# Block-sparse attention and a feed-forward layer: the elementwise work of h - tanh(h) divided anew over ScalarE, GpSimd and VectorE

## The chip, the core and the metric

The kernel runs on one core of a Trainium2 chip. A core has a matrix engine (TensorE, PE in the profile, with its weight loads as PEld), three engines for elementwise work (VectorE as DVE, ScalarE as ACT, GpSimd as POOL), and a queue for transfers (SyncE, SP). Each engine works through its own instructions in order and waits for others by semaphores. The metric is the time of the whole program on the device in microseconds; less is better. Before the change the median of 3 runs is 1019.51 us (1017.39 to 1022.18).

## What is computed

```python
# attention: q, k, v of shape (4, 8, 768, 64), blocks of 32 positions
scores = scale * np.matmul(q, k.transpose(0, 1, 3, 2))
scores = np.where(mask, scores, -1e9)          # band, first and last blocks, three sampled blocks
attn = softmax(scores)
x = np.matmul(attn, v)                         # then as 3072 tokens x 512
# feed-forward layer: w_in 512 x 2048, w_out 2048 x 512
h = x @ w_in
g = h - np.tanh(h)
out = g @ w_out
```

The weights come as 64-bit floats. All products are made nearly exact: each operand is split into a high and a low part, and three products of parts are added.

## The kernel before, in words

**The attention** fills the first 437 us. It goes through 16 pairs of heads, and in each head through 6 tiles of 128 keys. `load` fetches k, q and v of a pair (tiles rawk, rawq, rawv). `prep_v` finds the largest absolute value of v (am, L212), turns it into a scale and writes v in two parts (vhl, L230 and L231). `smax` makes the row maxima (sm, mc, L245 and L246), `qk_exp` the scores and their exponentials, `split` the two parts of these (ph, pl), `accum` the product with v. The results go to memory as x.

**The feed-forward layer** goes through six chunks of tokens: the first has 2 parts of 3 tiles of 128 tokens, four have 4 tiles, the last has 2. The 2048 columns of h come as 16 tiles of 128, numbered ft. One *unit* is one part of a chunk and one ft, so the first chunk has 32 units of 384 tokens, the next four 16 units of 512 each, the last 16 units of 256. `first` (L496) makes h of a unit in PSUM with 12 products and then g; `second` (L533) multiplies g with w_out, two units later (LAG = 2).

Between them stands the elementwise work. With u = h*h, h - tanh(h) is h*u*C(u) with a cubic C where u is at most 0.16 (THR2), and the plain difference elsewhere. u (L514), tanh (t, L516) and a square of the cubic (qq, L518) are made on ScalarE; the mask mk = u > 0.16 (L520) on GpSimd; the product g = h*u (L522), the difference t = tanh(h) - h (L523), the two factors of the cubic (L524, L525) and the selection by the mask (L526) on VectorE. Then ScalarE rounds g to its high part gh (L529) and GpSimd makes the low part gl = g - gh (L530). L522 and L523 read h from PSUM; L524 to L526, L520 and L530 have all their tensors in SBUF.

**The weights** of ft 0 to 2 are prepared during the attention. Those of ft 3 to 15 are fetched as 64-bit words during the first chunk into four staging tiles; `convert` makes 32-bit floats of them with three VectorE instructions for each of w_in and w_out (L415, L418, L421: cvti and cvto), and `split_w` their two parts, the high on ScalarE (L476), the low on GpSimd (L478).

**What sets the order.** The program gives each part of the attention a due time in units of key tiles and emits by it; the feed-forward layer is emitted step by step in `step` (L555). A scheduler with a model of the engines' times then moves instructions within each engine's order. Buffers come from pools with a fixed count for each name: f2 holds u, t, qq, mk and g twice, gh and gl three times; h has two PSUM banks.

Of the kernel before, what the change touches and what calls it, by code (L numbers as in the profile page):

```python
# [11 lines left out]
F32 = mybir.dt.float32  # L12
# [4 lines left out]
AF = mybir.ActivationFunctionType  # L17
ALU = mybir.AluOpType
# [31 lines left out]
NH0, H0, DH = 2, 12 * NPAIR, 2  # L50
X0, DX = 175, 2

# order of the attention's parts, in key tiles relative to the product of scores
TQK, TV, TSM, LSP, LAV = -15.1, -5.6, -10.3, 2.1, 4.2
HPH, HPL = 29, 30
RS, RQ, RV, HR = 1, 2.5, 3, 6
# [1 line left out]
PL_DVE_END = (2, 5, 8, 11)  # L58
PH_DVE = (4,)

# h - tanh(h) = h * u * C(u), u = h * h, with the cubic C factored, for u <= THR2
THR2 = 0.16
C3 = -0.01988785306343693
CR = 2.604505935007862
# [7 lines left out]
@with_exitstack  # L72
def attention_ffn(ctx, tc, q, k, v, samp, w_in, w_out, blocks, out):
    nc = tc.nc
    cst = ctx.enter_context(tc.tile_pool(name="cst", bufs=1))
    dpool = ctx.enter_context(tc.tile_pool(name="dpool", bufs=1, space=DRAM))
    xscr = [dpool.tile([P, T, DM], F32, name=f"xscr{b}") for b in range(B)]

    ident = cst.tile([P, P], F32, name="ident")
    make_identity(nc, ident)  # L80
    qbias = cst.tile([P, 1], F32, name="qbias")
    nc.vector.memset(qbias, QB)

    big = ctx.enter_context(tc.tile_pool(name="ps_big", bufs=3, space=PSUM))
    one = ctx.enter_context(tc.tile_pool(name="ps_one", bufs=2, space=PSUM))
    ps = (
        lambda name: big.tile([P, 1024], F32, tag="big", name=name),
        lambda name: one.tile([P, 512], F32, tag="one", name=name),
    )
    slots = [cst.tile([P, 4, 2, S], F32R, name=f"slot{i}") for i in range(NSLOT)]  # L90
    wt = {(m, ft): dpool.tile([P, 512], F32, name=f"w{m}{ft}") for ft in range(NPRE) for m in "io"}
    f2 = ctx.enter_context(tc.tile_pool(name="f2", bufs=2))
    ffn = FFN(tc, w_in, w_out, xscr, ident, qbias, ps, slots, wt, out, f2)
    with ExitStack() as actx:
        attention(actx, tc, q, k, v, samp, w_in, w_out, blocks, xscr, ident, ps, slots, wt, f2, ffn)
    with ExitStack() as fctx:
        ffn.rest(fctx)


def attention(ctx, tc, q, k, v, samp, w_in, w_out, blocks, xscr, ident, ps, slots, wt, f2, ffn):  # L100
# [4 lines left out]
    vhl = [acst.tile([P, 2, T, 129], F16, name=f"vhl{i}") for i in range(NV)]  # L105
    onesrow = acst.tile([1, P], F32, name="onesrow")

    # operands of the scores, stacked over the contraction, for both heads of a pair:
    # sA = [kh; mask; 1], sB = [qh; one-hot; -max], sC = [kl; kh], sD = [qh; ql]
    sA, sB, sC, sD = ([slots[i][:, x] for i in range(NSLOT)] for x in range(4))  # L110

    loads = {}

    # transfers that the start waits for: the first pair's high parts, its low parts, its maxima
    urgent = [[], [], []]

    def after(n, d):
# [5 lines left out]
    def load(pr, which="kqv", first=None):  # L123
        b, hp = divmod(pr, H // 2)
        r = loads.setdefault(pr, [])
        for nm, src in ((n, x) for n, x in (("k", k), ("q", q), ("v", v)) if n in which):
            t = p2.tile([P, 2, T, D], F32, tag="raw" + nm, name=f"raw{nm}{pr}", bufs=3 if nm == "v" else 2)
            d = nc.sync.dma_start(out=t, in_=src[b, 2 * hp : 2 * hp + 2].rearrange("h (p t) d -> p h t d", t=T))
# [6 lines left out]
    def setup():  # L135
        nc.vector.memset(onesrow, 1.0)
        for i in range(NV):
            nc.vector.memset(vhl[i][:, :, :, 64:65], 1.0)
        # additive mask of query block x key block, expanded to the key columns, on partitions 64..87
        R = slice(64, 88)  # L140
        sp_i = acst.tile([P, 6], I32, name="sp_i")
        nc.sync.dma_start(out=sp_i[R, :], in_=samp)
        st_sb = acst.tile([P, 2 * NB + S], F32, name="st_sb")
        nc.sync.dma_start(out=st_sb[R, :], in_=blocks)
        oh = st_sb[:, 2 * NB : 2 * NB + S]
        sp_f = acst.tile([P, 3], F32, name="sp_f")
        nc.vector.tensor_copy(out=sp_f[R, :], in_=sp_i[R, :].rearrange("p (j w) -> p j w", w=2)[:, :, 0])
        allow = st_sb[R, 0:NB]
        for j in range(3):
            nc.vector.scalar_tensor_tensor(  # L150
                out=allow, in0=st_sb[R, NB : 2 * NB], scalar=sp_f[R, j : j + 1], in1=allow, op0=ALU.is_equal, op1=ALU.max
            )
        neg = acst.tile([P, NB], F32, name="neg")
        nc.vector.tensor_scalar(out=neg[R, :], in0=allow, scalar1=1.0, scalar2=-MASKED, op0=ALU.subtract, op1=ALU.mult)
        nat = p2.tile([P, S], F32, tag="pe", name="nat", bufs=4)
        mk = p2.tile([P, S], F32, tag="pe", name="mk", bufs=4)
        nc.vector.tensor_copy(
            out=nat[R, :].rearrange("p (n j) -> p n j", j=BLK), in_=neg[R, :].unsqueeze(2).to_broadcast([NB, NB, BLK])
        )
        for i in range(NSLOT):  # L160
            nc.gpsimd.memset(sA[i].bitcast(F32)[64:89], 1.0)
        for r in range(2):
            nc.vector.tensor_copy(
                out=mk[R, r * HS : (r + 1) * HS].rearrange("p (u c) -> p u c", u=3),
                in_=nat[R, :].rearrange("p (c u r) -> p r u c", u=3, r=2)[:, r],
            )
        return oh, mk
# [158 lines left out]
    ev = []  # L326

    def ramp(h, by):
        """how much less ahead a part is in the first heads"""
        return by * max(0, 1 - (h - 1) / HR) if h else 0  # L330

    def at(time, f, *args):
# [76 lines left out]


def convert(nc, pool, raw, name):
    """float64 words -> float32"""
    w = raw.rearrange("p (n w) -> p n w", w=2)
    t = pool.tile([P, 512], I32, tag="wcvt", name=name)
    nc.vector.tensor_scalar(  # L415
# [9 lines left out]


def split_x(nc, src, pt, xh, xl, ident):
    """the transpose of a tile of tokens, in high and low parts"""
    for c in range(NCT):
        nc.tensor.transpose(pt[:, c * P : (c + 1) * P], src[:, c * P : (c + 1) * P], ident)  # L430
    ptv = pt.rearrange("p (c n) -> p c n", c=NCT)
    nc.scalar.activation(out=xh, in_=ptv, func=AF.Copy)
    nc.vector.tensor_tensor(out=xl, in0=ptv, in1=xh.bitcast(F32), op=ALU.subtract)
# [7 lines left out]
class FFN:  # L441
    LAG = 2

    def __init__(self, tc, w_in, w_out, xscr, ident, qbias, ps, slots, wt, out, f2):
        self.nc = tc.nc
        self.tc = tc
        self.w_in, self.w_out, self.xscr, self.ident, self.qbias, self.wt, self.out, self.f2 = (
            w_in, w_out, xscr, ident, qbias, wt, out, f2
        )  # fmt: skip
        self.big, self.one = ps  # L450
        self.wi = [[None] * NFT, [None] * NFT]
        self.wo = [[None] * NFT, [None] * NFT]
        flat = [slots[(NPAIR - 3 + x) % NSLOT].rearrange("p a j s -> p (a j s)") for x in range(3)]
# [24 lines left out]
            eng.tensor_tensor(out=lo, in0=t, in1=hi.bitcast(F32), op=ALU.subtract)  # L478

    def fetch_x(self, n, j):  # L480
        """a tile of tokens of chunk n, loaded as it is"""
        if n == 1:
            raw = self.f2.tile([P, DM], F32, tag="wcvt", name=f"xn{n}_{j}")
        else:
# [11 lines left out]
    def first(self, n, s, ft):  # L496
# [13 lines left out]
        def tl(tag, dt=F32, **kw):  # L510
            return f2.tile([P, 512], dt, tag=tag, name=f"{tag}{n}_{s}_{ft}", **kw)[:, 0:w_]

        u = tl("u")
        nc.scalar.activation(out=u, in_=ph, func=AF.Square)  # L514
        t = tl("t")
        nc.scalar.activation(out=t, in_=ph, func=AF.Tanh)  # L516
        qq = tl("qq")
        nc.scalar.activation(out=qq, in_=u, func=AF.Square, scale=QS, bias=self.qbias)  # L518
        mk = tl("mk")
        nc.gpsimd.tensor_scalar(out=mk, in0=u, scalar1=THR2, scalar2=None, op0=ALU.is_gt)  # L520
        g = tl("g")
        nc.vector.tensor_tensor(out=g, in0=ph, in1=u, op=ALU.mult)  # L522
        nc.vector.tensor_tensor(out=t, in0=t, in1=ph, op=ALU.subtract)  # L523
        nc.vector.scalar_tensor_tensor(out=g, in0=u, scalar=CR, in1=g, op0=ALU.subtract, op1=ALU.mult)  # L524
        nc.vector.scalar_tensor_tensor(out=g, in0=qq, scalar=QC, in1=g, op0=ALU.add, op1=ALU.mult)  # L525
        nc.vector.copy_predicated(g, mk.bitcast(I32), t)  # L526
# [27 lines left out]

    def step(self):  # L555
        n, s, ft = self.units.pop(0)
        if s == 0:
            if n == 0 and ft + 2 < NFT and ft:
                self.split_w(ft + 2)
            if n == 0 and ft and ft + AHEAD < NFT:  # L560
                self.fetch_w(ft + AHEAD)
        nx = sum(CHUNKS[n + 1]) if n + 1 < len(CHUNKS) else 0
        if n and ft == 5:
            for j in range(nx):
# [1 line left out]
        if n and 0 <= ft - XF < nx:  # L566
            self.turn_x(n + 1, ft - XF)
        self.pend.append((n, s, ft, *self.first(n, s, ft)))
        if n == 0 and ft == NFT - 1:
            js = [j for j in range(nx) if j // 2 == s]  # L570
            for j in js:
                self.fetch_x(1, j)
# [56 lines left out]
```

## Time and profile before

| | |
|---|---|
| median of 3 runs | 1019.51 us (1017.39 to 1022.18) |
| span of the profiled execution, first to last instruction | 1019.9 us |
| the profiled execution's own time | 1019.9 us; the span is all that the profile gives of it |
| PE busy | 948.4 us, 93% |
| DVE busy | 786.0 us, 77% |
| ACT busy | 590.9 us, 58% |
| POOL busy | 637.0 us, 62% |

By stage, in busy us of the stretch:

| stretch (us) | what | PE | DVE | ACT | POOL |
|---|---|---|---|---|---|
| 0 to 437 | attention | 393.21 | 360.21 | 330.48 | 302.95 |
| 440 to 614 | first chunk | 151.79 | 156.77 | 76.87 | 126.30 |
| 614 to 962 | four chunks of 512 | 348.00 | 226.35 | 158.37 | 177.59 |
| 962 to 1020 | last chunk | 52.40 | 41.69 | 25.12 | 27.88 |

Busy means that an instruction had started and not ended, so time in which it stood still inside counts as busy. The granted TensorE clock is 0.98 to 1.00 of full speed in all four stretches.

### The profile page before, as it was taken

Reading aid. Unit: us, or ns where it says so; the run is one execution under the profiler, and the core shown is the slowest. Engines: PE = TensorE matmul, PEld = TensorE weight load, DVE = VectorE, ACT = ScalarE, POOL = GpSimd, SP = SyncE. Lnnn points to the kernel's source line nnn. Section 1 sums busy time; section 2 is a strip of 40 time slices with the busy share of each in tenths; the row PEclk is TensorE's granted clock in tenths of the full one; section 3 lists DMA queues with packets and bytes.
Section 4 is the critical chain, followed back from the end, with each engine's and each line's share of the span. In section 5 each row is a group of like instructions: output and inputs, shape, how many; then the busy total and the mean of one; then the engine's idle time right before and its main releaser. Section 6 shows DMA issues by size and latency. Waiting matters only on the chain.

```text
span 1019.9 us, 19428 instructions
## 1 busy us (share of the span) xinstructions
PE 948.4 (93%) x7472; PEld 795.2 (78%) x7472; DVE 786.0 (77%) x1261; ACT 590.9 (58%) x926; POOL 637.0 (62%) x436
## 2 busy tenths in 40 slices
PE   5888999999999999897888899999999999999997
PEld 3667877888788888785766678888888888888896
DVE  5689887878788888979899987666666756666676
ACT  1665887888888888744344444445444534543453
POOL 1564777777778777866877866545455544544554
PEclk9997999999999999999899999999999999999999
DMA  7987687777766757133233121011000100000010
GB/s 193 252 223 205 144 175 151 157 173 169 159 157 156 156 131 183 48 120 105 81 114 92 43 93 52 1 42 42 21 5 17 63 1 1 31 11 1 1 42 22
DMA packets 73549, 97.75 MB, mean 96 GB/s; under 512 B 5880, under 2 KB 63416, under 8 KB 73456
## 3 DMA queue, kind: packets, MB, share of 16 engines
q1 hardware_dynamic: 73456, 96.51, 37.4%
q8 instruction: 59, 0.97, 0.4%
q14 instruction: 34, 0.28, 0.1%
HBM read 43.59 MB, written 14.16 MB: 57 GB/s over the span
## 4 chain that ended last, share of the span: by engine, by line
PE 64%; DVE 18%; DMA 8%; issue 5%; ACT 2%; POOL 1%; SPq 1%; POOLq 0%; DVEq 0%; ACTq 0%
PE h L507 21%; PE o L545 7%; PE o L543 7%; PE o L544 7%; PE st L269 5%; PE sm L245 5%; PE st L270 4%; DMA slot<-hiq 4%; PE av L299 2%; DVE g L524 2%; PE av L306 2%; PE av L305 2%; DMA slot<-nm 2%; DVE rs L316 2%; DVE mc L246 2%
## 5 line engine op out<-in xcount | busy, mean ns | idle before, releaser
L284 POOL TENSOR_TENSOR pl<-pe,ph 128x768 f16<-128x768 f32 x173 | 294.8, 1721 | 132.6 <-ACT ph L282 98.1
L530 POOL TENSOR_TENSOR gl<-g,gh 128x512 fp32r<-128x512 f32 (+2 forms) x112 | 135.1, 1209 | 191.6 <-ACT gh L529 191.3
L246 DVE TENSOR_REDUCE mc<-sm 128x1 f32<-128x768 f32 x192 | 181.6, 950 | 49.6 <-PE sm L245 48.4
L272 ACT ACTIVATE pe<-st 128x768 f32<-128x768 f32 x192 | 154.4, 805 | 77.3 <-PE st L270 72.8
L529 ACT ACTIVATE gh<-g 128x512 fp32r<-128x512 f32 (+2 forms) x112 | 63.9, 571 | 219.8 <-DVE g L526 210.6
L520 POOL TENSOR_SCALAR mk<-u 128x512 f32<-128x512 f32 (+2 forms) x112 | 160.9, 1436 | 46.6 <-ACT u L514 39.8
L522 DVE TENSOR_TENSOR g<-h,u 128x512 f32<-128x512 f32 (+2 forms) x112 | 68.4, 611 | 127.1 <-ACT t L516 115.8
L269 PE MATMUL st<-slot 128*128 128x512 f32 (+1 forms) x384 | 145.4, 379 | 8.8 <-DVE mc L246 4.8
L282 ACT ACTIVATE ph<-pe 128x768 f16<-128x768 f32 x168 | 141.7, 843 | 4.5
L270 PE MATMUL st<-slot 89*128 89x512 f32 (+1 forms) x384 | 128.7, 355 | 4.9 <-DMA slot<-nm 4.9
L299 PE MATMUL av<-vhl,ph 128*128 128x65 f16 x1152 | 130.2, 195 | 0.6 <-DVE sc L220 0.6
L245 PE MATMUL sm<-slot 88*128 88x512 f32 (+1 forms) x384 | 114.6, 385 | 16.7 <-DMA slot<-hiq 12.5
L305 PE MATMUL av<-vhl,ph 128*128 128x64 f16 x1152 | 130.0, 196 | 0.0
L306 PE MATMUL av<-vhl,pl 128*128 128x65 f16 x1152 | 128.2, 194 | 0.1
L306 PEld LDWEIGHTS <-pl 128*128 128x128 f16 x1152 | 107.9, 100 | 10.8 <-issue 6.8
L299 PEld LDWEIGHTS <-ph 128*128 128x128 f16 x1152 | 108.3, 98 | 4.6 <-issue 1.1
L305 PEld LDWEIGHTS <-ph 128*128 128x128 f16 x1152 | 108.9, 98 | 2.3 <-issue 1.6
L543 PE MATMUL o<-wx,gh 128*128 128x512 f32 x240 | 96.0, 400 | 7.9 <-ACT gh L529 6.9
L507 PE MATMUL h<-slot,wx 128*128 128x384 f32 (+1 forms) x480 | 102.5, 363 | 0.5 <-DVE t L523 0.5
L269 PEld LDWEIGHTS st<-slot 128*128 128x128 f32 x384 | 76.0, 198 | 28.9 <-DVE mc L246 7.4
L545 PE MATMUL o<-wx,gl 128*128 128x512 f32 x240 | 92.0, 398 | 4.9 <-POOL gl L530 4.7
L514 ACT ACTIVATE u<-h 128x512 f32<-128x512 f32 (+2 forms) x112 | 59.7, 533 | 62.8 <-PE h L507 52.4
(108 smaller groups left out, 2021.8 us busy)
## 6 DMA issues: line engine op xcount, KB each, us to landing
slot<-hik SPq DMA_DIRECT2D x64, 192.0 KB
slot<-hiq SPq DMA_DIRECT2D x64, 192.0 KB
stage<-w_in SPq DMA_DIRECT2D x13, 512.0 KB
stage<-w_out SPq DMA_DIRECT2D x13, 512.0 KB
rawk<-k SPq DMA_DIRECT2D x16, 384.0 KB
rawq<-q SPq DMA_DIRECT2D x16, 384.0 KB
slot<-lok SPq DMA_DIRECT2D x32, 192.0 KB
slot<-loq SPq DMA_DIRECT2D x32, 192.0 KB
```

What stands on the lines that cost most here:

```text
L245: nc.tensor.matmul(pm[:, c], lhsT=sB[s][0:88, j, t * P : (t + 1) * P], rhs=sA[s][0:88, j, c], start=True, stop=True)
L246: nc.vector.tensor_reduce(out=mcs[h][:, t : t + 1], in_=pm[:, 0:S], op=ALU.max, axis=AX.X)
L269: nc.tensor.matmul(st[:, c], lhsT=sC[s][:, j, kc], rhs=sD[s][:, j, c], start=True, stop=False)
L270: nc.tensor.matmul(st[:, c], lhsT=sA[s][0:89, j, kc], rhs=sB[s][0:89, j, c], start=False, stop=True)
L284: d = eng.tensor_tensor(out=pl, in0=pe, in1=ph, op=ALU.subtract)
L299: m = nc.tensor.matmul(o[:, to, :], lhsT=ph[:, c], rhs=vv[:, 0:65], start=(kt == 0 and t == 0), stop=False, skip_group_check=True)
L305: nc.tensor.matmul(o[:, to, 0:64], lhsT=ph[:, c], rhs=vv[:, 65:129], start=False, stop=False, skip_group_check=True)
L306: nc.tensor.matmul(o[:, to, :], lhsT=pl[:, c], rhs=vv[:, 0:65], start=False, stop=last, skip_group_check=True)
L507: nc.tensor.matmul(ph, lhsT=w[:, cc], rhs=x[:, c, tk], start=(k == 0), stop=(k == 3 * NCT - 1))
L520: nc.gpsimd.tensor_scalar(out=mk, in0=u, scalar1=THR2, scalar2=None, op0=ALU.is_gt)
L543: nc.tensor.matmul(o, lhsT=gh[:, c], rhs=wo[0][ft], start=(ft == 0), stop=False)
L545: nc.tensor.matmul(o, lhsT=gl[:, c], rhs=wo[0][ft], start=False, stop=(ft == NFT - 1))
```

## The change

Six things change.

1. The mask is no longer a comparison on GpSimd but ReLU(u - 0.16) on ScalarE, with the bias in a new tile tbias. A positive number is not zero, so its bits select as before.
2. ScalarE also copies h from PSUM to SBUF: into a new tile hs for the first part of the first chunk (s = 0), into g's own tile in every other unit.
3. GpSimd makes g = h*u from that copy; VectorE's L522 is gone.
4. In the units of the first part of the first chunk, GpSimd also makes t = tanh(h) - h from hs; elsewhere VectorE makes it from PSUM as before.
5. `split_w(ft + 2)` is called after `first` of the second part of an ft instead of before `first` of its first part.
6. hs needs 2 x 384 floats of each partition (pool fh); the tile rawv of the attention has 2 buffers instead of 3.

```diff
-            t = p2.tile([P, 2, T, D], F32, tag="raw" + nm, name=f"raw{nm}{pr}", bufs=3 if nm == "v" else 2)
+            t = p2.tile([P, 2, T, D], F32, tag="raw" + nm, name=f"raw{nm}{pr}", bufs=2)
...
+    tbias = cst.tile([P, 1], F32, name="tbias")
+    nc.vector.memset(tbias, -THR2)
...
+    fh = ctx.enter_context(tc.tile_pool(name="fh", bufs=2))
...
         u = tl("u")
         nc.scalar.activation(out=u, in_=ph, func=AF.Square)
+        g = tl("g")
+        turn = n == 0 and s == 0
+        hs = self.fh.tile([P, w_], F32, tag="hs", name=f"hs{n}_{s}_{ft}") if turn else g
+        nc.scalar.activation(out=hs, in_=ph, func=AF.Copy)
         t = tl("t")
         nc.scalar.activation(out=t, in_=ph, func=AF.Tanh)
         qq = tl("qq")
-        nc.scalar.activation(out=qq, in_=u, func=AF.Square, scale=QS, bias=self.qbias)
+        nc.scalar.activation(out=qq, in_=u, func=AF.Square, scale=QS, bias=qbias)
         mk = tl("mk")
-        nc.gpsimd.tensor_scalar(out=mk, in0=u, scalar1=THR2, scalar2=None, op0=ALU.is_gt)
-        g = tl("g")
-        nc.vector.tensor_tensor(out=g, in0=ph, in1=u, op=ALU.mult)
-        nc.vector.tensor_tensor(out=t, in0=t, in1=ph, op=ALU.subtract)
+        nc.scalar.activation(out=mk, in_=u, func=AF.Relu, bias=tbias)
+        nc.gpsimd.tensor_tensor(out=g, in0=hs, in1=u, op=ALU.mult)
+        if turn:
+            nc.gpsimd.tensor_tensor(out=t, in0=t, in1=hs, op=ALU.subtract)
+        else:
+            nc.vector.tensor_tensor(out=t, in0=t, in1=ph, op=ALU.subtract)
...
     def step(self):
         n, s, ft = self.units.pop(0)
-        if s == 0:
-            if n == 0 and ft + 2 < NFT and ft:
-                self.split_w(ft + 2)
-            if n == 0 and ft and ft + AHEAD < NFT:
-                self.fetch_w(ft + AHEAD)
+        if s == 0 and n == 0 and ft and ft + AHEAD < NFT:
+            self.fetch_w(ft + AHEAD)
...
         self.pend.append((n, s, ft, *self.first(n, s, ft)))
+        if s == 1 and n == 0 and ft and ft + 2 < NFT:
+            self.split_w(ft + 2)
```

In the changed file the lines of `first` stand a little lower: u L519, the copy of h L523, tanh L525, qq L527, mk L529, h*u L530, the difference on GpSimd L532 and on VectorE L534, the cubic L535 and L536, the selection L537, gh L540, gl L541; the splits' low part is L482.

**GpSimd in the first chunk**, before: one ft, from the low part of unit (s 0, ft 8) on. A name such as gl_0_8 is the tile gl of part 0 and ft 8; the number behind it is the buffer's.

```order
L530 TENSOR_TENSOR gl_0_8_8690<-g_0_8_8683,gh_0_8_8689 128x384
L520 TENSOR_SCALAR mk_0_9_8775<-u_0_9_8769 128x384
L530 TENSOR_TENSOR gl_1_8_8730<-g_1_8_8723,gh_1_8_8729 128x384
L520 TENSOR_SCALAR mk_1_9_8815<-u_1_9_8809 128x384
L478 TENSOR_TENSOR wx_7959<-cvti_8742,wx_7958 128x512
L478 TENSOR_TENSOR wx_7961<-cvto_8748,wx_7960 128x512
L530 TENSOR_TENSOR gl_0_9_8784<-g_0_9_8777,gh_0_9_8783 128x384
```

And after, the same stretch:

```order
L541 TENSOR_TENSOR gl_0_8_8709<-g_0_8_8694,gh_0_8_8708 128x384
L530 TENSOR_TENSOR g_1_8_8736<-g_1_8_8736,u_1_8_8734 128x384
L530 TENSOR_TENSOR g_0_9_8791<-hs_0_9_8792,u_0_9_8789 128x384
L532 TENSOR_TENSOR t_0_9_8794<-t_0_9_8794,hs_0_9_8792 128x384
L482 TENSOR_TENSOR wx_7971<-cvti_8947,wx_7970 128x512
L482 TENSOR_TENSOR wx_7973<-cvto_8953,wx_7972 128x512
L541 TENSOR_TENSOR gl_1_8_8750<-g_1_8_8736,gh_1_8_8749 128x384
L541 TENSOR_TENSOR gl_0_9_8806<-g_0_9_8791,gh_0_9_8805 128x384
```

Each ft had two masks, two low parts and two splits; now it has two products, one difference, two low parts and two splits, every one an operation on two tensors.

**VectorE in the attention**, around the maximum am of the values of a later pair. Before:

```order
L212 TENSOR_REDUCE am_3298<-rawv_2324 128x1
L220 TENSOR_SCALAR sc_2341<-sc_2341 1x1
L246 TENSOR_REDUCE mc_2176<-sm_3_2264 128x1
L221 TENSOR_SCALAR sc_2341<-sc_2341 1x1
L280 CAST ph_4_2333<-pe_4_2258 128x768
L222 TENSOR_SCALAR sc_2341<-sc_2341 1x1
L225 TENSOR_SCALAR sc_2341<-sc_2341 1x1
L246 TENSOR_REDUCE mc_2176<-sm_4_2316 128x1
L246 TENSOR_REDUCE mc_2176<-sm_5_2352 128x1
L228 COPY sb_2348<-pa_2339 128x2
L246 TENSOR_REDUCE mc_2408<-sm_0_2409 128x1
L231 SCALAR_TENSOR_TENSOR vhl_97<-rawv_1363,sb_2348,vhl_97 128x12x64
```

After, from the same write of vhl (now L234) on:

```order
L234 SCALAR_TENSOR_TENSOR vhl_102<-rawv_1368,sb_2353,vhl_102 128x12x64
L249 TENSOR_REDUCE mc_2413<-sm_0_2414 128x1
L256 TENSOR_SCALAR nm_2363<-pmt_2361 6x128
L317 TENSOR_SCALAR rs_2494<-av_2284 128x6
L318 RECIPROCAL rs_2494<-rs_2494 128x6
L249 TENSOR_REDUCE mc_2413<-sm_1_2429 128x1
L319 TENSOR_SCALAR rs_2494<-rs_2494,sb_1871 128x6
L215 TENSOR_REDUCE am_3303<-rawv_2329 128x1
```

The read of rawv into am stood eleven rows ahead of the write of vhl for an earlier pair; now it stands seven rows behind it, and its buffer is the one that this write sets free.

**ScalarE in a chunk of 512 tokens**, before, two units:

```order
L529 ACTIVATE gh_0_7_9755<-g_0_7_9749 128x512
L514 ACTIVATE u_0_8_9784<-h_0_8_9771 128x512
L516 ACTIVATE t_0_8_9786<-h_0_8_9771 128x512
L518 ACTIVATE qq_0_8_9788<-u_0_8_9784,qbias 128x512
L529 ACTIVATE gh_0_8_9798<-g_0_8_9792 128x512
```

After, one unit and the start of the next:

```order
L540 ACTIVATE gh_0_5_9728<-g_0_5_9715 128x512
L519 ACTIVATE u_0_6_9757<-h_0_6_9744 128x512
L523 ACTIVATE g_0_6_9759<-h_0_6_9744 128x512
L525 ACTIVATE t_0_6_9761<-h_0_6_9744 128x512
L527 ACTIVATE qq_0_6_9763<-u_0_6_9757,qbias 128x512
L529 ACTIVATE mk_0_6_9765<-u_0_6_9757,tbias 128x512
L540 ACTIVATE gh_0_6_9772<-g_0_6_9759 128x512
L519 ACTIVATE u_0_7_9801<-h_0_7_9788 128x512
```

In both, gh of a unit stands ahead of u of the next one here; copy and mask are two rows more for each unit.

More of the change, by code (lines that the diff above doesn't have):

```diff
@@ L92, in attention_ffn @@
     f2 = ctx.enter_context(tc.tile_pool(name="f2", bufs=2))
-    ffn = FFN(tc, w_in, w_out, xscr, ident, qbias, ps, slots, wt, out, f2)
+    fh = ctx.enter_context(tc.tile_pool(name="fh", bufs=2))
+    ffn = FFN(tc, w_in, w_out, xscr, ident, (qbias, tbias), ps, slots, wt, out, f2, fh)
     with ExitStack() as actx:
@@ L442, with __init__ @@
     LAG = 2
-    def __init__(self, tc, w_in, w_out, xscr, ident, qbias, ps, slots, wt, out, f2):
+    def __init__(self, tc, w_in, w_out, xscr, ident, bias, ps, slots, wt, out, f2, fh):
         self.nc = tc.nc
         self.tc = tc
-        self.w_in, self.w_out, self.xscr, self.ident, self.qbias, self.wt, self.out, self.f2 = (
-            w_in, w_out, xscr, ident, qbias, wt, out, f2
+        self.w_in, self.w_out, self.xscr, self.ident, self.bias, self.wt, self.out, self.f2 = (
+            w_in, w_out, xscr, ident, bias, wt, out, f2
         )
         self.big, self.one = ps
+        self.fh = fh
         self.wi = [[None] * NFT, [None] * NFT]
@@ L511, in tl @@
             return f2.tile([P, 512], dt, tag=tag, name=f"{tag}{n}_{s}_{ft}", **kw)[:, 0:w_]
+        qbias, tbias = self.bias
         u = tl("u")
         nc.scalar.activation(out=u, in_=ph, func=AF.Square)
+        g = tl("g")
+        turn = n == 0 and s == 0
+        hs = self.fh.tile([P, w_], F32, tag="hs", name=f"hs{n}_{s}_{ft}") if turn else g
+        nc.scalar.activation(out=hs, in_=ph, func=AF.Copy)
         t = tl("t")
```

## The prediction

> **What bounds the kernel now.** I read the stretches first (start:end in us, length, busy time of TensorE, its weight loads, DVE, ACT and POOL with instruction counts, then granted clock, DMA share and GB/s):
>
> ```profile
> 300.00:400.00 100.00, 95.85 (x1271) 83.29 (x1271) 85.27 (x146) 85.26 (x109) 77.01 (x47) 1.00 0.68 155
> 520.00:560.00 40.00, 35.29 (x162) 28.23 (x162) 39.21 (x59) 15.08 (x32) 31.40 (x23) 1.00 0.34 104
> 660.00:750.00 90.00, 90.00 (x410) 74.47 (x409) 58.33 (x88) 41.25 (x73) 44.56 (x33) 1.00 0.10 30
> ```
>
> The attention (300:400) and the feed-forward chunks of 512 tokens (660:750, TensorE busy 90.00 of 90) are bound by TensorE. The first chunk, two parts of 384 tokens (520:560), is not: DVE is busy 39.21 of 40 us, TensorE waits. Only there can a new division of elementwise work gain much. So the timeline of that chunk comes next, rows of DVE and POOL and two of TensorE's (start, duration, engine, line, operation):
>
> ```profile
> 541.54 0.68 DVE L418 SCALAR_TENSOR_TENSOR cvto<-stage,cvto 128x512 int32<-128x512 int32 x1
> 541.69 1.40 POOL L530 TENSOR_TENSOR gl<-g,gh 128x384 fp32r<-128x384 f32 x1 [0.43 <-ACT gh L529]
> 542.14 0.54 DVE L522 TENSOR_TENSOR g<-h,u 128x384 f32<-128x384 f32 x1
> 542.61 0.54 DVE L523 TENSOR_TENSOR t<-t,h 128x384 f32<-128x384 f32 x1
> 543.06 1.71 POOL L520 TENSOR_SCALAR mk<-u 128x384 f32<-128x384 f32 x1
> 543.07 0.68 DVE L421 SCALAR_TENSOR_TENSOR cvto<-stage,cvto 128x512 int32<-128x512 int32 x1
> 543.67 0.85 DVE L524 SCALAR_TENSOR_TENSOR g<-u,g 128x384 f32<-128x384 f32 x1
> 544.43 4.35 PE L507 MATMUL h<-slot,wx 128*128 128x384 f32 x24
> ...
> 544.75 1.29 POOL L478 TENSOR_TENSOR wx<-cvti,wx 128x512 fp32r<-128x512 f32 x1
> 545.38 1.08 DVE L525 SCALAR_TENSOR_TENSOR g<-qq,g 128x384 f32<-128x384 f32 x1
> 545.99 1.61 POOL L478 TENSOR_TENSOR wx<-cvto,wx 128x512 fp32r<-128x512 f32 x1
> 546.38 1.64 DVE L524 SCALAR_TENSOR_TENSOR g<-u,g 128x384 f32<-128x384 f32 x1
> 547.95 0.41 DVE L415 TENSOR_SCALAR cvti<-stage 128x512 int32<-128x512 int32 x1
> 548.28 0.58 DVE L526 COPY_PREDICATED g<-mk,t 128x384 f32<-128x384 int32 x1
> 548.76 0.54 DVE L525 SCALAR_TENSOR_TENSOR g<-qq,g 128x384 f32<-128x384 f32 x1
> ...
> 555.26 4.35 PE L507 MATMUL h<-slot,wx 128*128 128x384 f32 x24
> ```
>
> The pattern repeats every 555.26 - 544.43 = 10.83 us: one ft, that is two units of 384 tokens and the conversion of one pair of weight tiles. L525 takes 0.54 us alone and 1.08 while POOL runs a split; L524 takes 1.64 and ends at 548.02, 0.42 after the split ended (547.60). The other way round, the split that started at 545.99 ends 1.14 after DVE's L525 (546.46), and gl ends at 543.09, 0.87 after DVE's L418 (542.22). So a POOL operation on two tensors and a DVE operation that reads SBUF alone do not run together: each waits for the other's end. L522 and L523, which read h from PSUM, keep their 0.54 while gl runs. **The bound of this chunk is the time in which DVE and POOL exclude each other, not DVE's busy time.** The mask compare mk costs less: L524 beside it took 0.85, so 0.31 more, and was done (544.52) before mk (544.77).
>
> **The exclusive time of one ft, before and after.** A DVE instruction starts about 0.08 before the one ahead ends, so it occupies its duration less 0.08: 0.46 for L524 or L525, about 0.48 for L526, 0.60 for L418 or L421, 0.33 for L415, 0.47 for L522 or L523. On the pair that excludes, one ft needs from DVE 4 x 0.46 + 2 x 0.48 + 2 x (0.33 + 0.60 + 0.60) = 5.86. From POOL it needs now two gl and two splits, 2 x 0.87 + 2 x 1.14 = 4.02. A DVE instruction behind a POOL one saves 0.04 (0.42 for 0.46): 4 x 0.04 = 0.16. Two mk cost 2 x 0.31 = 0.62. Together 10.34 of the 10.83; 0.49 is idle.
>
> The change takes off DVE L522 twice and L523 once per ft, 3 x 0.47 = 1.41. None of that excludes POOL. It puts on POOL three products of two tensors per ft (h*u twice, tanh(h)-h once) and takes the two mk away. I price each at gl's 0.87: same engine, operation, shape and kind of operands. After: 5.86 + 5 x 0.87 + 2 x 1.14 - 7 x 0.04 = 12.21 us, **1.87 more than 10.34**. Bounds: no idle at all gives 12.21 - 10.83 = +1.38 per ft; twice the idle of now (the product now stands between two ACT steps, and POOL hands back to DVE) gives 12.21 + 0.98 - 10.83 = +2.36. I keep the idle of 0.49: 12.70, +1.87. Thirteen weight pairs are converted in this chunk (ft 3 to 15): **+24 us, +18 to +31**. That the conversions are issued at another place changes no sum: each still needs its 3.06 on DVE and 2.28 on POOL, and the new order even moves them nearer the start, where they meet the added products.
>
> Three of the 16 ft's carry no conversion. The last three now take (613.78 - 581.82) / 3 = 10.65 each:
>
> ```profile
> 581.82 0.47 ACT L514 ACTIVATE u<-h 128x384 f32<-128x384 f32 x1
> 613.78 0.60 ACT L514 ACTIVATE u<-h 128x512 f32<-128x512 f32 x1 [1.02 <-PE h L507]
> ```
>
> After, the exclusive time of such an ft is 4 x 0.46 + 2 x 0.48 + 5 x 0.87 - 5 x 0.04 = 6.95. TensorE needs more: 4.35 for 24 products, and 18 of 512 columns at 0.227 (5.44 / 24, units of a later chunk, below), 4.09, so 8.44. That could save 3 x 2.2 = 6.6; the last ft also waits for the next chunk's tokens, so I take 4 (0 to 7). First chunk: 24 - 4 = **+20, between +11 and +31**.
>
> **ACT** gets two operations per unit, priced by one like them on the same tiles (group of the stretch 523 to 588, with the mean in ns):
>
> ```profile
> L516 ACT ACTIVATE t<-h 128x384 f32<-128x384 f32 x12 | 5.8, 484 | 0.0
> ```
>
> The copy of h and the ReLU at 0.48 each are 1.9 us per ft on an engine busy 15.08 of 40. Hidden, at nothing; the cover is the wait of gh for DVE.
>
> **Chunks of 512 tokens.** One unit now, rows of ACT, POOL and DVE:
>
> ```profile
> 743.83 0.60 ACT L514 ACTIVATE u<-h 128x512 f32<-128x512 f32 x1 [0.18 <-PE h L507]
> ...
> 744.99 1.50 POOL L520 TENSOR_SCALAR mk<-u 128x512 f32<-128x512 f32 x1
> 746.15 0.69 DVE L524 SCALAR_TENSOR_TENSOR g<-u,g 128x512 f32<-128x512 f32 x1
> 746.94 0.69 DVE L525 SCALAR_TENSOR_TENSOR g<-qq,g 128x512 f32<-128x512 f32 x1
> 747.73 0.76 DVE L526 COPY_PREDICATED g<-mk,t 128x512 f32<-128x512 int32 x1
> 748.52 0.63 ACT L529 ACTIVATE gh<-g 128x512 fp32r<-128x512 f32 x1 [3.00 <-DVE g L526]
> 749.24 1.30 POOL L530 TENSOR_TENSOR gl<-g,gh 128x512 fp32r<-128x512 f32 x1 [2.74 <-ACT gh L529]
> 749.27 0.60 ACT L514 ACTIVATE u<-h 128x512 f32<-128x512 f32 x1
> ```
>
> Units follow at 749.27 - 743.83 = 5.44, TensorE's own pace. After, the product on POOL follows the last unit's gl, which ends 1.27 behind u (749.24 + 1.30 - 749.27), and ends 2.55 behind u; then 0.05, two steps of 0.79, 0.76, 0.03, gh 0.63 and 0.12 to the next u: 5.72. That is 0.28 over the pace wherever ACT keeps gh ahead of the next u. The new order puts the next u ahead of gh several times in each chunk, and the second product runs two units behind, so the lag is caught up. Taken at 0. The last chunk of 256 tokens: 0, within 2 either way.
>
> **The v buffer.** With two buffers a load of v starts only when the one two pairs earlier has been used:
>
> ```profile
> 258.60 1.69 DVE L231 SCALAR_TENSOR_TENSOR vhl<-rawv,sb,vhl 128x768 f16<-128x768 f32 x1
> ...
> 260.32 0.37 SPq L128 DMA_DIRECT2D rawv<-v  x1
> ```
> ```profile
> 64.11 7.02 DMA rawi<-w_in
> ...
> 444.99 3.04 DMA xscr<-xq
> ```
> ```profile
> L246 DVE TENSOR_REDUCE mc<-sm 128x1 f32<-128x768 f32 x192 | 181.6, 950 | 49.6 <-PE sm L245 48.4
> ```
>
> DVE now reads that v (am) after only two mc and four small instructions, 2 x 0.95 and about 0.8, so 2.7 us. A transfer of the same 384 KB took 3.04 with the queues quiet, one of 512 KB 7.02 under load. DVE, in order, would stand 0.3 to 4.3 us in each of some 14 pairs, with mc, and so TensorE, behind it. DVE has 15 us of 100 free there; I take +1 in all (0 to +20).
>
> **Sum**, against the profiled span of 1019.9 (the median of the runs shown is 1019.51, so it stands for them): 1019.9 + 20 + 1 = 1040.9, less 0.4 for the median, rounded: **1040 us**.
>
> **Rivals.**
> *DVE's queue is the bound.* For it: 39.21 of 40 busy. If POOL's spans stretched without stopping DVE, an ft would lose 1.41: 13 x 1.41 + 4 = 22, **997 us**. Against it: 1.08 and 1.64 where 0.54 was due.
> *The mask compare excludes DVE as fully as gl does.* It would end 544.77 - 543.75 = 1.02 behind DVE, so an ft has 5.86 + 4.02 + 2 x 1.02 - 0.24 = 11.68 now, and the change adds only 0.53: 13 x 0.53 - 4 + 1 = +4, **1023 us**. Against it: L524 at 746.15 kept 0.69 inside mk (744.99 to 746.49), and 11.68 is over the 10.83 measured.
> The Trainium skill (SBUF — State Buffer, SBUF: two separate sides) says that DVE with two SBUF inputs and GpSimd take one pair of ports as an exclusive lock for the whole instruction. By that rule mk would hold it like gl, and the time would be this rival's 1023; the trace agrees for gl and the splits (1.64 for 0.54) and not for mk (0.69 kept).
> *The wait moves to the v buffer* and takes the place of nothing: a stall of 3 us, of which TensorE loses half, in 14 pairs adds 20: **1060 us**. It decides from the point where the load lands over 3 us later than 2.7. For: the later load; against: the queues are quiet when it starts.
> *The chain in the 512-token units decides*: 64 units x 0.28 = 18, **1058 us**, if the reordered places do not catch up.
>
> **Numbers.** Forecast 0.55 (its own range 1030 to 1052), DVE bound 0.12, mask excludes 0.11, v buffer 0.12, chain 0.10. Within 0.5%, about what a measurement here can tell from no change, lies the third alone: same 0.11. Faster 0.12, slower 0.77. The range, 1014 to 1060, leaves out the faster case and little more.
>
> **What would show it.** In the new profile of the first chunk: POOL busy over 90% of it, L535 and L536 often near 1.4 us, the period of an ft with conversion near 12.7, DVE's own busy time including its stalls still high. The 512-token chunks keep TensorE at 100% with units at 5.44. In the attention am waits for its load under 1 us. I am wrong if h*u on POOL runs beside DVE's chain without stretching it, or if the ft falls below 10.8.

## The result and the profile after

The changed kernel takes 1045.57 us (median of 4 runs, 1042.89 to 1048.37); the kernel before, run beside it, 1020.85 (4 runs, 1017.39 to 1025.74). The ratio is **1.0243, 95% interval 1.0207 to 1.0279**: slower. The forecast was 1040, with a range of 1014 to 1060. The profiled execution has a span of 1046.6 us, against 1019.9 before.

First the stretches of the four stages, cut at the first u of each stage. Columns: start:end in us, length, busy time (instructions) of TensorE, its weight loads, DVE, ACT and POOL, then granted clock, DMA share, GB/s. Before:

```profile
0.00:440.00 440.00, 396.21 (x4849) 338.34 (x4850) 361.20 (x590) 330.50 (x422) 305.25 (x186) 0.97 0.70 164
440.00:613.80 173.80, 151.59 (x753) 123.58 (x751) 156.77 (x247) 76.67 (x161) 126.30 (x90) 0.98 0.31 97
613.80:964.00 350.20, 350.20 (x1578) 290.00 (x1577) 228.14 (x341) 158.57 (x277) 178.19 (x127) 1.00 0.06 20
964.00:1019.90 55.90, 50.40 (x300) 43.30 (x298) 39.90 (x84) 25.12 (x68) 27.28 (x33) 0.99 0.08 29
```

After (the attention ends at 442.5; the last row is a piece of the first chunk):

```profile
442.50:639.70 197.20, 155.98 (x755) 128.84 (x752) 170.37 (x199) 104.56 (x224) 136.56 (x107) 0.95 0.27 86
639.70:989.50 349.80, 349.80 (x1576) 289.64 (x1575) 214.96 (x275) 223.62 (x405) 167.43 (x127) 1.00 0.06 20
989.50:1046.60 57.10, 50.73 (x301) 43.45 (x299) 37.98 (x70) 35.28 (x100) 26.23 (x33) 0.97 0.08 29
530.00:570.00 40.00, 28.09 (x129) 22.20 (x127) 39.42 (x43) 20.08 (x43) 30.33 (x23) 1.00 0.29 93
```

The stages moved by +2.5 (attention), **+23.4 (first chunk, 173.8 to 197.2)**, -0.4 (the four chunks of 512 tokens) and +1.2 us (last chunk). In the first chunk DVE has 48 instructions fewer, 199 for 247, and is busy 13.6 us longer: it stands still inside instructions. The granted clock of TensorE is 0.95 in this chunk, against 0.98 before, but TensorE is busy for only 155.98 of the 197.20 us, 4.4 us more than before, so its clock does not explain the 23.4. The timeline of DVE and POOL there, as in the prediction (start, duration, engine, line, operation):

```profile
555.44 1.19 POOL L530 TENSOR_TENSOR g<-g,u 128x384 f32<-128x384 f32 x1
555.68 1.50 DVE L424 SCALAR_TENSOR_TENSOR cvti<-stage,cvti 128x512 int32<-128x512 int32 x1
556.60 1.45 POOL L530 TENSOR_TENSOR g<-hs,u 128x384 f32<-128x384 f32 x1
557.11 1.49 DVE L421 SCALAR_TENSOR_TENSOR cvto<-stage,cvto 128x512 int32<-128x512 int32 x1
558.01 1.44 POOL L532 TENSOR_TENSOR t<-t,hs 128x384 f32<-128x384 f32 x1
558.63 1.37 DVE L424 SCALAR_TENSOR_TENSOR cvto<-stage,cvto 128x512 int32<-128x512 int32 x1
559.41 1.73 POOL L482 TENSOR_TENSOR wx<-cvti,wx 128x512 fp32r<-128x512 f32 x1
559.92 0.54 DVE L534 TENSOR_TENSOR t<-t,h 128x384 f32<-128x384 f32 x1
560.38 1.17 DVE L535 SCALAR_TENSOR_TENSOR g<-u,g 128x384 f32<-128x384 f32 x1
561.10 1.59 POOL L482 TENSOR_TENSOR wx<-cvto,wx 128x512 fp32r<-128x512 f32 x1
561.58 1.52 DVE L536 SCALAR_TENSOR_TENSOR g<-qq,g 128x384 f32<-128x384 f32 x1
```

Read the ends, start plus duration: POOL 556.63, DVE 557.18, POOL 558.05, DVE 558.60, POOL 559.45, DVE 560.00, POOL 561.14, DVE 561.55, POOL 562.69, DVE 563.10. The two engines work strictly in turn: 0.55 for a conversion on DVE, 0.87 and 0.85 for the product and the difference that are new on POOL, 1.14 for a split, 0.41 for a factor of the cubic. Only L534, which reads h from PSUM, takes part in no turn: 0.54, inside a split.

The period of an ft follows from the rows of u, two for each ft. These are the u of the first ft, of the fourteenth, and the first of the next chunk; before:

```profile
439.98 0.49 ACT L514 ACTIVATE u<-h 128x384 f32<-128x384 f32 x1 [3.66 <-PE h L507]
```

After:

```profile
442.53 0.49 ACT L519 ACTIVATE u<-h 128x384 f32<-128x384 f32 x1 [2.85 <-PE h L511]
...
605.34 0.49 ACT L519 ACTIVATE u<-h 128x384 f32<-128x384 f32 x1
...
639.73 0.60 ACT L519 ACTIVATE u<-h 128x512 f32<-128x512 f32 x1 [2.33 <-PE h L511]
```

In the kernel before, the other two stand at 581.82 and 613.78 (shown in the prediction). So the first thirteen ft's take (605.34 - 442.53) / 13 = 12.52 us each, against (581.82 - 439.98) / 13 = 10.91 before: 21.0 us more in all. The last three take (639.73 - 605.34) / 3 = 11.46, against 10.65: 2.4 us more. Their stretches, before and after:

```profile
581.82:613.78 31.96, 29.85 (x141) 23.96 (x142) 25.57 (x41) 15.65 (x34) 20.37 (x16) 1.00 0.26 84
605.34:639.73 34.39, 32.05 (x156) 26.27 (x155) 21.08 (x30) 19.69 (x45) 17.59 (x17) 1.00 0.20 69
```

### The profile page after: what moved, and what is told of

The parts are those of the page before. It is cut to its first block, busy times and chain, and to the rows that moved or that the text cites. A ratio compares the mean times of both kernels' runs of the same rounds, so it can differ in the third digit from the quotient of the medians.

```text
span 1046.6 us, 19457 instructions
## 1 busy us (share of the span) xinstructions
PE 953.1 (91%) x7472; PEld 798.9 (76%) x7472; DVE 796.3 (76%) x1134; ACT 695.1 (66%) x1150; POOL 635.5 (61%) x452
## 4 chain that ended last, share of the span: by engine, by line
PE 56%; DVE 25%; DMA 8%; issue 6%; POOL 2%; ACT 1%; SPq 1%; DVEq 0%; POOLq 0%; ACTq 0%
PE h L511 18%; PE o L554 6%; PE o L556 6%; PE o L555 6%; PE st L272 5%; PE sm L248 5%; PE st L273 4%; DVE mc L249 3%; DVE g L535 3%; DVE rs L319 3%; DMA rawv<-v 2%; DVE g L537 2%; DVE g L536 2%; PE av L302 2%; PE av L309 2%
## 5 line engine op out<-in xcount | busy, mean ns | idle before, releaser
L541 POOL TENSOR_TENSOR gl<-g,gh 128x512 fp32r<-128x512 f32 (+2 forms) x112 | 136.6, 1222 | 173.8 <-ACT gh L540 170.5
L540 ACT ACTIVATE gh<-g 128x512 fp32r<-128x512 f32 (+2 forms) x112 | 64.2, 574 | 149.9 <-DVE g L537 142.9
L530 POOL TENSOR_TENSOR g<-g,u 128x512 f32<-128x512 f32 (+2 forms) x96 | 117.8, 1227 | 74.1 <-ACT g L523 74.0
L534 DVE TENSOR_TENSOR t<-t,h 128x512 f32<-128x512 f32 (+2 forms) x96 | 59.3, 618 | 120.1 <-ACT t L525 119.9
L273 PE MATMUL st<-slot 89*128 89x512 f32 (+1 forms) x384 | 126.5, 350 | 0.0
L535 DVE SCALAR_TENSOR_TENSOR g<-u,g 128x512 f32<-128x512 f32 (+2 forms) x112 | 99.0, 885 | 29.2 <-POOL g L530 28.2
L511 PE MATMUL h<-slot,wx 128*128 128x384 f32 (+1 forms) x480 | 107.6, 373 | 10.8 <-DVE t L534 10.8
L511 PEld LDWEIGHTS h<-slot,wx 128*128 128x128 f32 x480 | 90.7, 195 | 23.1 <-DVE t L534 12.9
```

The lines of the kernel that those rows point to most:

```text
L273: nc.tensor.matmul(st[:, c], lhsT=sA[s][0:89, j, kc], rhs=sB[s][0:89, j, c], start=False, stop=True)
L511: nc.tensor.matmul(ph, lhsT=w[:, cc], rhs=x[:, c, tk], start=(k == 0), stop=(k == 3 * NCT - 1))
```

## The experiments

All edits are made to the kernel before, except where the text says that they are made to the changed one. A ratio is to the kernel before on the same chip, with its 95% interval. Stage times are those of the profiled execution, cut as above.

### The parts of the change, one at a time

**The product on GpSimd.** ScalarE copies h, GpSimd multiplies; the mask stays on GpSimd.

```diff
-        nc.vector.tensor_tensor(out=g, in0=ph, in1=u, op=ALU.mult)
+        nc.scalar.activation(out=g, in_=ph, func=AF.Copy)
+        nc.gpsimd.tensor_tensor(out=g, in0=g, in1=u, op=ALU.mult)
```

> One part alone: the kernel before with h copied by ScalarE and the product h*u on GpSimd; the mask stays a compare on GpSimd, the difference and the conversions as before. Exclusion: each product adds 0.87 less 0.04 to the exclusive time, 1.66 per ft, so +22 to +27 us, ratio 1.021 to 1.027. DVE's queue as the bound: DVE loses 0.94 per ft, ratio 0.985.

Measured: 1052.34 us, 1.0295 (1.0247 to 1.0344); first chunk 200.3. That is a little above what was expected, and more than the whole change costs. This one move carries the loss. In its profile all conversions are made by 569 us, and from 570 us to the end of the chunk TensorE is busy 69.28 of 71.30 us. So the turns of DVE and POOL bind the first part of the chunk there, and TensorE the rest.

**The mask on ScalarE.**

```diff
-        nc.gpsimd.tensor_scalar(out=mk, in0=u, scalar1=THR2, scalar2=None, op0=ALU.is_gt)
+        nc.scalar.activation(out=mk, in_=u, func=AF.Relu, bias=tbias)
```

> One part alone: the kernel before with the mask as ReLU(u - 0.16) on ScalarE, nothing else moved. If what binds the first chunk is the time in which DVE and POOL exclude each other and a mask compare costs 0.31 of it, an ft loses up to 0.62 us: 16 x 0.62 = 10, so a ratio of 0.990 to 1.000 to the kernel before. If DVE's queue is the bound: 1.000, since no DVE instruction goes. If the compare excludes as fully as gl (1.02 each), an ft loses 2.04 until TensorE binds: 0.975 to 0.98.

Measured: 1025.77 us, 1.0035 (1.0005 to 1.0065); first chunk 178.2, so 4.4 longer. A miss: work was taken off GpSimd, and there was no gain. DVE and POOL of this run:

```profile
540.17 0.55 DVE L524 TENSOR_TENSOR g<-h,u 128x384 f32<-128x384 f32 x1
540.64 0.54 DVE L525 TENSOR_TENSOR t<-t,h 128x384 f32<-128x384 f32 x1
542.38 1.21 POOL L532 TENSOR_TENSOR gl<-g,gh 128x384 fp32r<-128x384 f32 x1 [2.68 <-ACT gh L531]
542.64 1.24 DVE L417 TENSOR_SCALAR cvto<-stage 128x512 int32<-128x512 int32 x1
543.78 1.71 POOL L480 TENSOR_TENSOR wx<-cvti,wx 128x512 fp32r<-128x512 f32 x1 [0.19 <-ACT wx L478]
544.27 1.78 DVE L420 SCALAR_TENSOR_TENSOR cvto<-stage,cvto 128x512 int32<-128x512 int32 x1
545.97 0.55 DVE L524 TENSOR_TENSOR g<-h,u 128x384 f32<-128x384 f32 x1
```

(Lines stand two lower here: L524 and L525 are the two that read h.) They run at 540.17 to 541.18, when POOL has nothing to do: it waits 2.68 for gh. gl and the split fall on conversions instead, 1.24 for 0.41 and 1.78 for 0.68. Half an ft takes 545.97 - 540.17 = 5.80 us: DVE's own 3.87 and these two stalls of 0.83 and 1.10, in all 5.80. DVE is never idle here. So the period is **DVE's own queue plus those POOL operations that do not lie beside a DVE instruction that reads PSUM**. Before, one ft is 7.74 of DVE's own (the 5.86 and the four times 0.47 of the prediction) and 3.09 of stalls, of which mk made 0.62. POOL's gl and splits of 4.02 cost 2.47 of it; the rest lay beside L522 and L523. Without mk the order on POOL shifts, that cover is lost, and the stalls are 3.86. (The 3.09 holds some 0.2 of idle time, and the 0.62 is the prediction's price for mk, which the doubled mask below puts higher.) The chunk as a whole grew by less than this even stretch would give, since its first six ft's took 56.5 us, against 64.0 before.

**Two buffers of v.**

```diff
-            t = p2.tile([P, 2, T, D], F32, tag="raw" + nm, name=f"raw{nm}{pr}", bufs=3 if nm == "v" else 2)
+            t = p2.tile([P, 2, T, D], F32, tag="raw" + nm, name=f"raw{nm}{pr}", bufs=2)
```

> One part alone: the kernel before with two buffers for v in the attention instead of three. The changed kernel reached the first chunk 2.6 us later, with 12.6 us of waits of DVE for v; if that is this part, the ratio is 1.002 to 1.004. If the later v were the main loss, 1.015 or more. If the 2.6 us came from elsewhere, 1.000.

Measured: 1018.21 us, 0.9972 (0.9944 to 0.9999); attention 438.9, against 440.0. It costs nothing. The loads do come late, in the waits by operation (total us, times, longest):

```profile
DVE am L212 <- DMA rawv<-v: 7.5, 5, 4.7
```

Before, this row read 3.5, 1, 3.5. These waits do not reach the end; DVE, busy 85.27 of 100 us in the attention before, has room for them.

**The conversions emitted later** (`split_w(ft + 2)` behind `first` of the second part, as in the change).

> One part alone: the kernel before with the conversions called after the products of the second part of an ft. Exclusion counts the same instructions, so 1.000. If the place of the conversions is a loss of its own (they queue ahead of the difference that frees a PSUM bank), 1.005 to 1.015.

Measured: 1019.76 us, 0.9976 (0.9955 to 0.9997); first chunk 175.1. As expected, it moves nothing that counts.

### What the price is made of

**The product stays on VectorE, but reads the copy of h in SBUF.** This takes away the PSUM read and gives POOL nothing.

```diff
-        nc.vector.tensor_tensor(out=g, in0=ph, in1=u, op=ALU.mult)
+        nc.scalar.activation(out=g, in_=ph, func=AF.Copy)
+        nc.vector.tensor_tensor(out=g, in0=g, in1=u, op=ALU.mult)
```

> The port alone: the kernel before with h copied by ScalarE, the product h*u still on DVE, but read from the copy in SBUF instead of PSUM. DVE's and POOL's instruction counts stay. Exclusion: the product of 0.46 now excludes POOL, 0.92 per ft more than 10.34, of which 0.49 was idle: +0.4 to +0.9 per ft, +7 to +15 us, ratio 1.007 to 1.015. DVE's queue as the bound: 1.000.

Measured: 1043.41 us, 1.0194 (1.0138 to 1.0249); first chunk 193.0, **19.2 longer, with the same number of DVE and POOL instructions per ft**. Rows of it (L478 is a split, L523 the product):

```profile
541.97 1.77 POOL L478 TENSOR_TENSOR wx<-cvti,wx 128x512 fp32r<-128x512 f32 x1
542.53 1.63 DVE L523 TENSOR_TENSOR g<-g,u 128x384 f32<-128x384 f32 x1
544.08 0.54 DVE L524 TENSOR_TENSOR t<-t,h 128x384 f32<-128x384 f32 x1
```

The product took 0.54 to 0.56 before in all 32 units, whatever POOL did; from SBUF this one waits for the split's end and takes 1.63. So the product joins the exclusion. DVE's 247 instructions of this chunk are busy 170.03 us, against 156.77: 13.3 of the 19.2 us are standing still inside instructions, near the 16 x 0.92 = 14.7 that the sum of exclusive times gives if nothing of it falls into idle time. The other 5.9 us are idle time of DVE: it waits 15.9 us for ScalarE's copy (DVE g L523 <- ACT g L522), where the product before waited 6.0 us for ScalarE. That the product also covers no POOL operation any more is argued from the rows of the mask's run above; this run does not separate it from the wait for the copy.

**The difference back on VectorE** (on the changed kernel, with three buffers of v and no hs).

```diff
-        turn = n == 0 and s == 0
+        turn = False
```

> The changed kernel with two parts undone: the difference tanh(h) - h on DVE from PSUM in every unit, and three buffers for v. Exclusion: POOL loses 0.87 less 0.04 per ft, 16 x 0.83 = 13 us, and the attention 2.6: against the kernel before a ratio of about 1.009 to 1.013 instead of 1.024. If the moved differences cost nothing, 1.021 (the attention alone).

Measured: 1040.72 us, 1.0187 (1.0153 to 1.0221); first chunk 192.4 for 197.2. So the difference on GpSimd costs 4.8 us by these two profiles, far less than was expected, and not nothing. With DVE's queue always full, the move takes 0.47 off DVE and puts 0.87 - 0.04 of exclusive time in its place: 0.36 per ft, 16 x 0.36 = 5.8.

This run also shows what the mask is worth beside the moved product. It differs from the run with the product alone (first chunk 200.3) by the mask on ScalarE, the place of the copy in ScalarE's order, and the later conversions (1.3 us longer by themselves): 192.4 is 7.9 less. So the move that gained nothing alone (4.4 longer) seems to gain here, and the parts of this change do not simply add up one by one.

**The mask twice** (a second, identical comparison in the first chunk).

```diff
+        if n == 0:
+            nc.gpsimd.tensor_scalar(out=mk, in0=u, scalar1=THR2, scalar2=None, op0=ALU.is_gt)
```

> The mask compare is made twice on GpSimd in the units of the first chunk, the same result both times. If a compare costs DVE 0.31, an ft grows by up to 0.62: 0 to +10 us, ratio 1.000 to 1.010, a little more if POOL's own queue fills up. If a compare excludes DVE for 1.02: 2.04 per ft, +33 us, ratio 1.032.

Measured: 1036.24 us, 1.0129 (1.0082 to 1.0176); first chunk 188.6, 14.8 longer: above the 10 us of the one expectation and half of the 33 of the other. A comparison of this run and the two DVE instructions beside it:

```profile
557.37 1.61 POOL L520 TENSOR_SCALAR mk<-u 128x384 f32<-128x384 f32 x1
557.88 0.85 DVE L526 SCALAR_TENSOR_TENSOR g<-u,g 128x384 f32<-128x384 f32 x1
558.65 0.54 DVE L524 TENSOR_TENSOR g<-h,u 128x384 f32<-128x384 f32 x1
```

Again 0.85 for 0.54, and DVE's L526 ends at 558.73, before mk does at 558.98. A comparison costs 14.8 / 32 = 0.46 us on average, where the prediction had 0.31. The Trainium skill (SBUF — State Buffer, SBUF: two separate sides) would have mk hold the ports for its whole length; neither this row nor the 14.8 agrees, while the turns of the operations on two tensors do agree.

### The other direction

**Mask on ScalarE, and the low parts of the converted weights on VectorE**, so that GpSimd keeps only gl in the first chunk (the mask's edit as above, and):

```diff
-            eng = nc.vector if ft < 2 and x else nc.gpsimd
+            eng = nc.vector if (ft < 2 and x) or ft >= NPRE else nc.gpsimd
```

> A candidate: the kernel before with the mask on ScalarE and the low parts of the 26 converted weight tiles made on DVE instead of GpSimd. Exclusion: a split takes 0.60 of DVE in place of 1.14 of POOL, so an ft needs 5.86 + 1.20 + 2 x 0.87 - 0.08 = 8.72 in place of 10.34, while DVE's own queue holds 7.74 + 1.20 = 8.94 and still waits for gl: 9.4 to 10.2 per ft, ratio 0.98 to 0.99. DVE's queue as the bound with its waits unchanged: +1.2 per ft, ratio 1.015.

Measured: 1010.53 us, 0.9900 (0.9863 to 0.9938); first chunk 168.7. DVE has two instructions more per ft, and the kernel is faster. What is left:

```profile
549.46 2.26 POOL L532 TENSOR_TENSOR gl<-g,gh 128x384 fp32r<-128x384 f32 x1 [7.04 <-ACT gh L531]
549.72 0.68 DVE L420 SCALAR_TENSOR_TENSOR cvto<-stage,cvto 128x512 int32<-128x512 int32 x1
550.32 0.58 DVE L528 COPY_PREDICATED g<-mk,t 128x384 f32<-128x384 int32 x1
551.76 0.56 DVE L524 TENSOR_TENSOR g<-h,u 128x384 f32<-128x384 f32 x1 [0.85 <-POOL gl L532]
```

This gl takes 2.26. It got its turn only when DVE had nothing more to run, at 550.90, and DVE had nothing more because L524 waited for this gl: g has two buffers.

**The same with three buffers of g** (and two of v, to make the room, which cost nothing above).

```diff
-        g = tl("g")
+        g = tl("g", bufs=3)
```

> The candidate with the mask on ScalarE and the converted low parts on DVE, and in addition three buffers for g (paid by two for v). In that candidate DVE stood 0.86 us per ft before a product until gl of two units earlier had read the buffer. If that wait simply goes, an ft takes 9.0 to 10.2 us in place of 10.8 and the ratio to the kernel before is 0.975 to 0.988. If gl, kept off by DVE's uninterrupted work, only makes TensorE wait instead, 0.99 as without the buffer.

Measured: **996.21 us (5 runs, 991.91 to 998.71), 0.9753 (0.9727 to 0.9779)**, the fastest here, faster than both kernels. First chunk 147.3. A stretch and four rows:

```profile
530.00:570.00 40.00, 38.64 (x192) 33.64 (x191) 39.75 (x80) 27.55 (x57) 20.66 (x10) 1.00 0.22 67
```
```profile
539.48 2.15 POOL L532 TENSOR_TENSOR gl<-g,gh 128x384 fp32r<-128x384 f32 x1 [3.13 <-ACT gh L531]
540.68 0.55 DVE L524 TENSOR_TENSOR g<-h,u 128x384 f32<-128x384 f32 x1
541.15 0.54 DVE L525 TENSOR_TENSOR t<-t,h 128x384 f32<-128x384 f32 x1
...
549.65 0.56 DVE L524 TENSOR_TENSOR g<-h,u 128x384 f32<-128x384 f32 x1
```

gl still takes 2.15, but it ends at 541.63, with the two PSUM reads (540.68 to 541.69): it waits for them and lies beside them, and DVE stands nowhere. The period is 549.65 - 540.68 = 8.97, DVE's own 7.74 and two splits of 0.60, in all 8.94. TensorE is busy 38.64 of 40.

**GpSimd silent in the first chunk** (the edits before the last, and gl on VectorE there).

```diff
+        eng = nc.gpsimd if n else nc.vector
+        eng.tensor_tensor(out=gl, in0=g, in1=gh.bitcast(F32), op=ALU.subtract)
```

> The same candidate (mask on ScalarE, converted low parts on DVE) with gl of the first chunk on DVE too, so that GpSimd does nothing in that chunk. If exclusion is what stretches DVE's instructions, none is stretched now and an ft takes DVE's own queue, 8.94 + 2 x 0.47 = 9.88 us: ratio 0.98 to 0.988 to the kernel before, although DVE is given more work than ever. If the stretched durations come from DVE itself (its operands, not POOL), they stay, and an ft takes over 11.5: 1.01 or more.

Measured: 1012.6 us, 0.9901 (0.9867 to 0.9935), just outside what was expected; first chunk 161.8. A stretch, and the group of L526 (count, busy us, mean ns):

```profile
530.00:570.00 40.00, 34.41 (x161) 27.84 (x161) 40.00 (x82) 23.03 (x49) 0.00 (x0) 1.00 0.28 83
```
```profile
L526 DVE SCALAR_TENSOR_TENSOR g<-u,g 128x384 f32<-128x384 f32 x11 | 6.0, 546 | 0.0
```

With POOL at 0.00 no instruction of DVE stands still: L526, the first factor of the cubic, has a mean of 546 ns between 525 and 575 us, against 1184 for the same operation (L524) in the kernel before between 522 and 577. DVE is busy 40.00 of 40 and is now the bound itself; the first thirteen ft's take 9.97 each, where 9.88 was expected. The gap to the run before, 161.8 - 147.3 = 14.5, is close to what gl costs on DVE, 16 x 2 x 0.47 = 15.0. So the two ways in which the first chunk can be bound stand side by side: by the turns of DVE and POOL, or by DVE's own work.

## Why the prediction was right

| step | forecast | profile |
|---|---|---|
| attention, v buffer | +1 (0 to 20) | +2.5 |
| first chunk | +20 (11 to 31) | +23.4 |
| four chunks of 512 | 0 | -0.4 |
| last chunk | 0, within 2 | +1.2 |
| sum of the span | +21 | +26.7 |

**The bound and the sign: right, and shown.** DVE and POOL exclude each other in the first chunk. POOL silent gives unstretched DVE rows; the product on POOL alone gives 1.0295. The price of a product, 0.87 as gl's, is what the turns show (0.87, 0.85).

**The sum of an ft: nearly right, with terms that were wrong.** Over the first thirteen ft's the period is 12.52, where 12.70 was forecast: +21.0 us for +24. The sum counted exclusive time, 12.21, plus 0.49 of idle, and called the 1.41 taken off DVE's PSUM reads free of effect. DVE was not idle by 0.49 (busy 39.21 of 40, so about 0.2 per ft); the rest would be PSUM reads with no POOL operation beside them. The rule that fits the runs is DVE's own 7.74 - 1.41 = 6.33, plus POOL's 5 x 0.87 + 2 x 1.14 - 7 x 0.04 = 6.35, less a cover of at most 0.47 from the one read left: 12.21 to 12.68. The forecast's 12.70 lies just above its upper end. **The difference on GpSimd** was mis-sized: it stood for 0.83 per ft, 13.3 us over 16 ft's, and costs 4.8 us, 0.30 per ft. The mask stood for 0.62 saved per ft, 9.9 us; it saved nothing alone and some 7.9 us beside the moved product. The two products stood for 1.66 per ft, 26.6 us, and the run with the product alone took 26.5 more; but as TensorE binds the end of that chunk, this does not test the price of a single product.

**The last three ft's: wrong.** The forecast took 4 us off them, because they carry no conversion and TensorE alone would need 8.44 each; they took 2.4 us more. TensorE was already busy for 29.85 of their 31.96 us before, so at most 2.1 us were to be had. Nor were they free of conversions: most of DVE's work on the last pair, up to an L421 at 586.39, and its two splits lie in them, while in the changed kernel all splits end by 596.35, before they begin. TensorE has 156 instructions there, for 141 before, so some of its products came later; what moved them was not tried. That +23.4 came so near to +20 is in part luck: +21.0 for +24 and +2.4 for -4 are errors in opposite directions.

**The order of the conversions.** The thirteen pairs are split between 459 and 596 us, some ten ft's, so more than one pair falls on an ft there and the ft's are uneven. The argument that the place of the conversions changes no sum holds for the average, not for a single ft.

**The signs to look for.** L535 and L536 at 1.17 and 1.52, and an ft of 12.52: right. "POOL busy over 90%" was wrong: 136.56 of 197.2, 69%; POOL waits for gh while DVE has its turn, and the sign should have been named for DVE. "am waits under 1 us" was wrong too:

```profile
DVE am L215 <- DMA rawv<-v: 12.6, 6, 6.4
```

The load is late six times, as the rival of the v buffer said, but the experiment with two buffers shows no cost. So the +2.5 of the attention are not shown to come from it. The attention also took 442.9 in the run with the product from SBUF, whose edit leaves v alone, and 438.0 in the one with later conversions. What makes these 5 us of spread stays open.

**Chunks of 512 tokens: right.** The start of four units in a row there, by ACT's u:

```profile
703.61 0.58 ACT L519 ACTIVATE u<-h 128x512 f32<-128x512 f32 x1
...
709.28 0.58 ACT L519 ACTIVATE u<-h 128x512 f32<-128x512 f32 x1
...
714.95 0.58 ACT L519 ACTIVATE u<-h 128x512 f32<-128x512 f32 x1
...
719.44 0.60 ACT L519 ACTIVATE u<-h 128x512 f32<-128x512 f32 x1 [1.71 <-PE h L511]
```

Two units of 5.67 (the chain was put at 5.72), and one of 4.49 that makes up for them. TensorE is busy 349.80 of 349.80. The rival of the chain falls.

**The other rivals.** "DVE's queue is the bound" (997) falls for this kernel; it came true only where POOL was taken out of the way. "The mask excludes as fully" (1023) falls with the doubled comparison, though a mask costs half as much again as the prediction had. The row that the prediction named against it, L524 at 746.15, does not lie inside mk: it ends at 746.84, after mk's end at 746.49. It is weaker evidence than it looked, though its 0.69 shows no stall; the doubled comparison is what decides.

## What to carry to other kernels

Two engines that are each busy below 100% can still be one engine: compare the end of each instruction with the last end on the other engine, and if they follow in turn, add their work up instead of taking the larger. A VectorE instruction that reads PSUM was in no turn here and covered GpSimd's operations, so the product moved to GpSimd, or onto an SBUF copy, cost more for each unit (26.5 / 32 = 0.83 and 19.2 / 32 = 0.60 us) than the instruction's own 0.47 us. The difference, moved where DVE had such a read left, cost less (0.30). Before giving GpSimd more, try giving it less, and see that the buffer it releases is deep enough for it to wait for such a cover.

## What the runs showed of the hardware

- GpSimd can be kept waiting through several VectorE instructions in a row. In the run with the splits on VectorE one gl took 2.26 us, through L420 and L528, and the next one 1.02, since DVE's queue let it in at once; with three buffers of g it mostly took 2.14 to 2.43. The undisturbed one, from the run with the splits on VectorE:

```profile
552.16 1.02 POOL L532 TENSOR_TENSOR gl<-g,gh 128x384 fp32r<-128x384 f32 x1 [0.43 <-ACT gh L531]
```

- TensorE got a new wait, for the PSUM bank of h that L534 frees, when L534 stood behind stalled conversions (us in all, times, longest). In the kernel before, the same wait (for L523) is 0.7 us in all, 2 times. Here it follows from DVE's stalls and was not tried by itself:

```profile
PE h L511 <- DVE t L534: 14.0, 8, 3.1
```
